# Normalised rows stored by the attention and read through DMA transposes, in a kernel of two recurrent-attention and two gMLP blocks

## The chip, the cores and the metric

One core of one Trainium2 chip. The time is device microseconds (us) of the whole program, the median of its executions. Ratios are the mean time of one kernel's fast runs over that of the other's fast runs of the same rounds on the same chip, so they are not quite the ratio of the medians quoted beside them. The kernel before had medians from 2015 to 2028 us on six occasions, so kernels of different occasions are compared by their ratios to it. Where two kernels are compared stage by stage, that is from one profiled execution of each.

## The reference, cut to what matters

```python
def _A_ref(x, mem0, Wq, Wk, Wv, Wo, seg_len):     # attention over 64 segments of 32 rows, 32 heads of 128
    mem = mem0                                    # 8 memory rows, carried from segment to segment
    for s in range(n_seg):
        h = concat([mem, x[:, 32*s:32*s+32]])
        ...                                       # q, k, v, masked softmax, Wo
        mem = o[:, :M, :].copy()
        outs.append(o[:, M:, :])

def _B_ref(x, w_in, w_sp, b_sp, w_out):           # gMLP: S = 2048 rows, D = 512, F = 1376, Fh = 688
    z = _gelu(einsum('bsd,df->bsf', x, w_in))
    z1 = z[..., :Fh]
    z2 = _layernorm(z[..., Fh:])
    g = einsum('ts,bsf->btf', w_sp, z2) + b_sp
    return einsum('bsf,fd->bsd', z1 * g, w_out)

x = x + _A_ref(_layernorm(x), ...)                # block 1
x = x + _B_ref(_layernorm(x), ...)
x = x + _A_ref(_layernorm(x), ...)                # block 2, the same weights
x = x + _B_ref(_layernorm(x), ...)
```

## The kernel before

TensorE, VectorE and ScalarE run in program order; the order on GpSimd and on SP's DMA queue is a scheduler's. A block is: 64 attention segments; then 16 projections (a row tile of 128 rows is loaded, normalised, transposed, projected to 1376 columns; Gelu on ScalarE; statistics, reciprocal root and normalisation of z2 on VectorE); then 16 gate tiles. The attention's row sums (x plus attention output) are made during later segments, in groups of four row tiles, the last four in the gMLP.

```python
# attention, once per segment s = 4 * tb + j4; `spare` is called ahead of the output product
def spare():
    if ys:
        y_add(ys.pop(0))                               # VectorE: sum, statistics; SP: store to xd
    if tb % 4 == 3 and j4 == 1 and tb > 4:
        due.extend(range(tb - 7, tb - 3))
    if due:
        ys.append(due.pop(0))
        rows.y_load(ys[0], first)                      # SP: 1 + 8 loads for the next sum
    ...
    if j4 == 3 and tb + 2 < NB:
        rows.apply(tb + 2, MV_in, RS_in, first=first)  # VectorE: normalise; SP: 1 store, 4 + 4 reloads
...
# gMLP
def turn_x(tt):
    nc.gpsimd.tensor_scalar(out=_nat(xn[:]), in0=_perm(xt.pop(tt)[:]), ...)        # normalise
    for kt in range(KT):
        nc.tensor.transpose(pT[:, kt * P:(kt + 1) * P], xn[:, kt * P:(kt + 1) * P], ident_bf[:])
    nc.scalar.copy(xnT[tt][:].rearrange("p kt r -> p (kt r)"), pT[:, 0:512])
...
load_x(0); load_x(1)
for t in range(3):
    load_wsp(t)                                        # SP: DMA transposes of w_sp, 128 x 2048 each
turn_x(0)
for tt in range(NT):
    if tt + 2 < NT: load_x(tt + 2)                     # ScalarE's queue
    if tt + 1 < NT: turn_x(tt + 1)
    project(tt)
    if late: late.pop(0)()                             # last four row sums, on GpSimd
    if tt % 2 == 1:
        _rstd_dve(...); normalise(tt - 1); normalise(tt)
...
for t in range(NT):
    gate(t, range(0, 4))                               # each: columns 0:512 and 512:688
    if t > 0: turn_u(t - 1)
    gate(t, range(4, 12))
    if t > 0: finish(t - 1)
    gate(t, range(12, NT))
    product(t)
...
# start
c = _consts(ctx, tc, B_b_sp)                           # GpSimd builds identity and mask, VectorE casts them
...                                                    # then the rows, then the weights (GpSimd's queue)
```

The softmax here doesn't subtract the row's maximum and nothing guards it: scores larger than these inputs give would overflow.

Of the kernel before, what the change touches and what calls it, by code (L numbers as in the profile page):

```python
# [8 lines left out]
F32 = mybir.dt.float32  # L9
# [21 lines left out]
def _perm(ap):  # L31

    return ap.rearrange("p (cg kt el) -> p kt cg el", cg=4, kt=4, el=32)


def _nat(ap):
    return ap.rearrange("p (kt cg el) -> p kt cg el", kt=4, cg=4, el=32)


def _consts(ctx, tc, b_sp):  # L40
# [51 lines left out]
    nc.gpsimd.dma_start(bsp_bf[:], b_sp.rearrange("(t p) -> p t", p=P))  # L92
# [41 lines left out]
class _Rows:  # L134


    def __init__(self, nc, pool, c, xd, xn_d, oA_d, oB_d, x_in):
        self.nc, self.pool, self.c, self.xd, self.xn_d, self.oA_d, self.oB_d, self.x_in = nc, pool, c, xd, xn_d, oA_d, oB_d, x_in
        self.xs, self.preB, self.pre, self.y = {}, {}, {}, {}
# [26 lines left out]
    def y_load(self, tb, first):  # L166
        nc = self.nc
        xs = self.pool.tile([P, DM], BF16 if first else F32, name="y_xb" if first else "y_x")
        nc.sync.dma_start(xs[:], (self.x_in if first else self.xd)[tb * P:(tb + 1) * P, :])
        ot = self.pool.tile([P, 4, P], F32, name="y_o")  # L170
        for j in range(4):
            nc.sync.dma_start(ot[32 * j:32 * j + 24, :, :],
                              self.oA_d[4 * tb + j + 1].rearrange("(cg r) c -> r cg c", cg=4)[8:32])
            r0 = 32 * (tb % 4) + 8 * j
            nc.sync.dma_start(ot[32 * j + 24:32 * j + 32, :, :], self.oB_d[tb // 4, r0:r0 + 8, :].rearrange("r (cg c) -> r cg c", cg=4))
        self.y[tb] = (ot, xs)

    def y_add(self, tb, first, MV, eng):
        ot, xs = self.y.pop(tb)
        o = ot[:].rearrange("p cg c -> p (cg c)")  # L180
        eng.tensor_tensor(out=_perm(o) if first else o, in0=_perm(o) if first else o, in1=_nat(xs[:]) if first else xs[:], op=ALU.add)
        self.nc.sync.dma_start(self.xd[tb * P:(tb + 1) * P, :], o)
        _stats(self.nc, self.pool, o, MV[:, tb, :])


def b_block(tc, c, rows, xd, MV_in, RS_in, MV_out, RS_out, w_in, w_sp, w_out, S, late, out_final=None):
# [4 lines left out]
    with ExitStack() as ctx:  # L191
# [22 lines left out]
        def load_x(tt):  # L214
            xt[tt] = gp.tile([P, DM], F32, name="xs")
            nc.scalar.dma_start(xt[tt][:], xd[tt * P:(tt + 1) * P, :])

        def load_wsp(t):
            wsp[t] = wsp_pool.tile([P, NT, P], BF16, name="wspT")
            nc.sync.dma_start_transpose(out=wsp[t][:], in_=w_sp[t * P:(t + 1) * P, :].rearrange("t (st s) -> t st s", s=P))  # L220

        def turn_x(tt):
            xn = zp.tile([P, DM], BF16, name="xn")
            nc.gpsimd.tensor_scalar(out=_nat(xn[:]), in0=_perm(xt.pop(tt)[:]), scalar1=MV_in[:, tt, 0:1], scalar2=RS_in[:, tt:tt + 1],
                                    op0=ALU.subtract, op1=ALU.mult)
            pT = one.tile([P, 1024], BF16, name="pT")
            for kt in range(KT):
                nc.tensor.transpose(pT[:, kt * P:(kt + 1) * P], xn[:, kt * P:(kt + 1) * P], ident_bf[:])
            xnT[tt] = zp.tile([P, KT, P], BF16, name="xnT")
            nc.scalar.copy(xnT[tt][:].rearrange("p kt r -> p (kt r)"), pT[:, 0:512])  # L230
# [19 lines left out]
        load_x(0)  # L250
        load_x(1)
# [4 lines left out]
        turn_x(0)  # L256
        for tt in range(NT):
            if tt + 2 < NT:
                load_x(tt + 2)
            if tt + 1 < NT:  # L260
                turn_x(tt + 1)
            project(tt)
            if late:
                late.pop(0)()
            if tt % 2 == 1:
                _rstd_dve(nc, zp, RSz[:, tt - 1:tt + 1], MVz[:, tt - 1:tt + 1, 1], 2)
                normalise(tt - 1)
                normalise(tt)
# [6 lines left out]
        def gate(t, sts):  # L275
            if sts[0] == 0:
                pg[t] = big.tile([P, 1536], F32, name="pg")
            for st in sts:
                for c0, c1 in ((0, 512), (512, FH)):
                    nc.tensor.matmul(pg[t][:, c0:c1], lhsT=wsp[t][:, st, :], rhs=z2n[:, st, c0:c1], start=(st == 0), stop=(st == NT - 1))  # L280

        def product(t):
            del wsp[t]
            if t + 3 < NT:
                load_wsp(t + 3)
            u[t] = gp.tile([P, FH], BF16, name="u")
            nc.vector.scalar_tensor_tensor(out=u[t][:], in0=pg.pop(t)[:, 0:FH], scalar=c["bsp"][:, t:t + 1], in1=z1[:, t, :],
                                           op0=ALU.add, op1=ALU.mult)
            load_x(t)
# [10 lines left out]
        def finish(t):  # L300
            py = one.tile([P, DM], F32, name="py")
            for fc, (f0, fsz) in enumerate(FCH):
                nc.tensor.matmul(py[:], lhsT=uT[t][0:fsz, fc, :], rhs=w_out_sb[0:fsz, fc, :], start=(fc == 0), stop=(fc == 5))  # L303
            del uT[t]
            xs = xt.pop(t)
            if out_final is not None:
                xob = gp.tile([P, DM], BF16, name="xob", bufs=1)
                nc.vector.tensor_tensor(out=_nat(xob[:]), in0=_nat(py[:]), in1=_perm(xs[:]), op=ALU.add)
                nc.scalar.dma_start(out_final[t * P:(t + 1) * P, :], xob[:])
                return  # L310
            xo = gp.tile([P, DM], F32, name="xo", bufs=1)
            nc.vector.tensor_tensor(out=_perm(xo[:]), in0=_nat(py[:]), in1=_perm(xs[:]), op=ALU.add)
            nc.scalar.dma_start(xd[t * P:(t + 1) * P, :], xo[:])
            _stats(nc, zp, xo[:], MV_out[:, t, :])
            _rstd_act(nc, RS_out[:, t:t + 1], MV_out[:, t, 1:2], c)
            if t < 2:
                rows.apply(t, MV_out, RS_out, x=xo[:])

        for t in range(NT):
            gate(t, range(0, 4))  # L320
            if t > 0:
                turn_u(t - 1)
            gate(t, range(4, 12))
            if t > 0:
                finish(t - 1)
            gate(t, range(12, NT))
            product(t)
# [5 lines left out]
def kernel(  # L333
# [24 lines left out]
    c = _consts(ctx, tc, B_b_sp)  # L358
# [3 lines left out]
    xn_d = dram.tile([M + S, DM], BF16, name="xn_d")  # L362
    oA_d = dram.tile([S // SEG + 1, P, P], F32, name="oA_d")
# [3 lines left out]
    rows = _Rows(nc, rp, c, xd, xn_d, oA_d, oB_d, x_in)  # L367
    MV, RS = c["MV"], c["RS"]
    with tc.manual_schedule(engines=ORDERED):
# [10 lines left out]
        wqkv = a_open_qkv_weights(tc, ctx, A_Wq, A_Wk, A_Wv)  # L380
        for tt in range(2):
            _stats(nc, rp, rows.xs[tt][:], MV[0][:, tt, :])
            _rstd_act(nc, RS[0][:, tt:tt + 1], MV[0][:, tt, 1:2], c)
            rows.apply(tt, MV[0], RS[0], first=True)
    for blk in range(2):
        late = a_block(tc, c, rows, MV[0], RS[0], MV[1], RS[1], wqkv, A_Wo, S, first=(blk == 0))
        b_block(tc, c, rows, xd, MV[1], RS[1], MV[0], RS[0], B_w_in, B_w_sp, B_w_out, S, late, out_final=out2 if blk == 1 else None)
# [23 lines left out]
def a_block(tc, c, rows, MV_in, RS_in, MV_out, RS_out, wqkv, Wo, S, first):  # L411
# [6 lines left out]
    with ExitStack() as ctx:  # L418
# [123 lines left out]
        def y_add(tb):  # L542
            rows.y_add(tb, first, MV_out, nc.vector)
            copies.append(lambda: _rstd_act(nc, RS_out[:, tb:tb + 1], MV_out[:, tb, 1:2], c))
# [22 lines left out]
        def segment(s, fill, spare):  # L567
# [141 lines left out]
            run(turns)  # L709
            if s + 1 < NSEG:  # L710
                prep_segment(s + 1)
# [9 lines left out]
        for s in range(NSEG):  # L721
# [8 lines left out]
            def spare():  # L730
                if ys:
                    y_add(ys.pop(0))
                if tb % 4 == 3 and j4 == 1 and tb > 4:
                    due.extend(range(tb - 7, tb - 3))
                if due:
                    ys.append(due.pop(0))
                    rows.y_load(ys[0], first)
# [8 lines left out]
            segment(s, lambda: next(more, None), spare)  # L746
# [9 lines left out]
        for tb in ys + due:  # L756
            if tb in due:
                rows.y_load(tb, first)
            y_add(tb)
            run(copies)  # L760


    def late_rstd():
        _rstd_dve(nc, rows.pool, RS_out[:, NB - 4:NB], MV_out[:, NB - 4:NB, 1], 4)

    def step(tb):
        if tb > NB - 4:
            rows.y_add(tb - 1, first, MV_out, nc.gpsimd)
        if tb < NB:
            rows.y_load(tb, first)  # L770

    return [lambda tb=tb: step(tb) for tb in range(NB - 4, NB + 1)] + [late_rstd]
# [35 lines left out]
```

## Time and profile before

| | before |
|---|---|
| time | 2015.21 us (2015.08 to 2018.89) |
| busy: TensorE, VectorE, ScalarE | 89%, 62%, 52% |
| start, to attention segment 0 | 49.4 us |
| attention of block 1, of block 2 | 767.2, 768.3 us |
| projections of block 1, of block 2 (end of the attention's last product to the first gate's product) | 101.1, 102.2 us |
| gates and the turn to block 2; gates of block 2 | 119.2; 109.3 us |

The stages are cut at TensorE's first matmul on the rows of segment 0, at its last matmul of the attention (T), and at VectorE's first product u. The prediction shows the page's lines, the waits and the stage table that this rests on.

Two waits that the prediction did not read matter later, so here they are, from the waits of the whole execution before (total, times, longest):

```profile
DVE y_o L181 <- DMA y_o<-oB_d: 23.2, 3, 11.8
PE psm L452 <- DVE hA L560: 10.8, 12, 1.3
```

VectorE waits for the loads of a row sum (y_o) only three times (a fourth wait of 9.8 us is put down to the store of the attention's output). All four lie where an attention ends (at 810, 823, 1803 and 1812 us), and TensorE's wait for the next segment's rows (hA) is never longer than 1.3 us. So before, row sums don't hold up the segments.

### The profile page before, as it was taken

The numbers are of one execution on the slowest core, as the hardware profiler recorded it, in microseconds if no ns is written. First come the engines' busy times: TensorE is split into PE (matmuls) and PEld (weight loads), VectorE is DVE, ScalarE is ACT, GpSimd is POOL, SyncE is SP. The second block draws the span as 40 slices with busy tenths as digits, with TensorE's granted clock in tenths as the row PEclk, the third lists the DMA queues.
The fourth block names the chain that finished last, engine by engine and source line by source line (L and its number), as shares of the span: only waits on it lengthen the run. The fifth ranks groups of instructions, "written<-read, shape, count | busy, mean of one in ns | idle before, by whom it ended". The sixth has DMA issues, their size and how long they took to land.

```text
span 2016.6 us, 95153 instructions
## 1 busy us (share of the span) xinstructions
PE 1796.6 (89%) x43866; PEld 1027.9 (51%) x43904; DVE 1256.0 (62%) x2835; ACT 1047.8 (52%) x1888; POOL 166.9 (8%) x249
## 2 busy tenths in 40 slices
PE   1999999999999999558989999999999999976798
PEld 0555555555555555224545555555555555542354
DVE  1676777777778766264346676677766777643622
ACT  1566566666666655332236665666666665634311
POOL 5000000000000000440010000000000000014200
PEclk9999999999999999779999999999999999997899
DMA  8200000020012001625540000001200110035153
GB/s 294 77 23 17 19 17 17 24 66 21 17 31 63 18 15 37 176 65 128 150 134 24 20 21 20 20 21 42 65 28 22 56 54 16 16 113 141 52 142 100
DMA packets 163073, 120.09 MB, mean 60 GB/s; under 512 B 97088, under 2 KB 136272, under 8 KB 162672
## 3 DMA queue, kind: packets, MB, share of 16 engines
q1 hardware_dynamic: 141968, 65.71, 12.5%
q10 hardware_dynamic: 13840, 23.08, 3.7%
q0 software_dynamic: 6864, 25.21, 3.5%
q8 instruction: 343, 5.62, 1.2%
q14 instruction: 58, 0.48, 0.1%
HBM read 67.68 MB, written 29.50 MB: 48 GB/s over the span
## 4 chain that ended last, share of the span: by engine, by line
PE 63%; DVE 12%; ACT 10%; DMA 6%; issue 4%; POOL 2%; SPq 1%; DVEq 0%; POOLq 0%; ACTq 0%
PE psm L452 22%; PE pw L509 10%; PE psb L452 8%; PE pg L280 5%; DVE KA L588 5%; ACT rows L584 4%; ACT E L612 3%; PE psO L631 3%; PE psS L608 3%; DVE E L615 3%; PE pwB L518 2%; PE py L303 2%; PE pz L236 2%; DMA xs<-xd 2%; PE psM L675 2%
## 5 line engine op out<-in xcount | busy, mean ns | idle before, releaser
L452 PEld LDWEIGHTS <-hA 128*32 128x32 bf16 x12288 | 308.5, 96 | 307.9 <-DVE hA L560 47.1
L584 ACT CAST rows<-psm 128x512 bf16<-128x512 f32 x512 | 299.7, 585 | 191.2 <-PE psm L452 191.2
L509 PE MATMUL pw<-Wo_sb,uT 128*32 128x128 bf16 x16640 | 267.1, 220 | 32.1 <-issue 21.8
L452 PE MATMUL psm<-Wq_sb,hA 128*32 128x512 bf16 x4096 | 275.3, 384 | 11.3 <-DVE hA L560 10.8
L509 PEld LDWEIGHTS <-uT 128*32 128x32 bf16 x16640 | 245.2, 97 | 72.4 <-issue 33.8
L452 PE MATMUL psm<-Wk_sb,hA 128*32 128x512 bf16 x4096 | 270.4, 381 | 0.0
L452 PE MATMUL psv<-Wv_sb,hA 128*32 128x512 bf16 x4096 | 268.0, 382 | 0.0
L588 DVE STREAM_TRANSPOSE QQ<-rows 128x512 bf16<-128x512 bf16 x256 | 182.1, 711 | 93.3 <-ACT rows L584 92.0
L647 DVE TENSOR_TENSOR uT<-psO,Rt 128x384 bf16<-128x384 f32 x256 | 138.1, 539 | 128.7 <-ACT Rt L637 128.7
L588 DVE STREAM_TRANSPOSE KA<-rows 128x512 bf16<-128x512 bf16 x256 | 182.2, 712 | 40.7 <-ACT rows L584 35.9
L612 ACT ACTIVATE E<-psS 128x448 bf16<-128x448 f32 x256 | 140.0, 547 | 107.6 <-PE psS L608 107.6
L594 DVE CAST VA<-psv 128x512 bf16<-128x512 f32 x256 | 175.6, 686 | 2.3
L553 POOL COPY QQ<-QTB 128x256 bf16<-128x256 bf16 x128 | 51.1, 401 | 1407.9 <-PE psS L608 846.6
L280 PE MATMUL pg<-z2n,wspT 128*128 128x176 bf16 (+1 forms) x1002 | 158.9, 308 | 4.0 <-DVE z2n L247 2.2
L608 PEld LDWEIGHTS <-KA 128*64 128x64 bf16 x2048 | 79.7, 113 | 127.8 <-DVE KA L588 127.4
L637 ACT ACTIVATE Rt<-Rt 128x1024 f32<-128x1024 f32 x128 | 135.3, 1057 | 4.1
L452 PEld LDWEIGHTS <-hB 128*32 128x32 bf16 x3072 | 75.8, 97 | 106.5 <-DVE hB L467 37.3
L636 ACT ACTIVATE Rt<-psD 128x1024 f32<-128x1024 f32 x128 | 128.6, 1004 | 0.0
L692 DVE TENSOR_TENSOR uT<-psO,Rm 128x128 bf16<-128x128 f32 x256 | 62.7, 286 | 92.5 <-PE psO L631 92.4
L608 PE MATMUL psS<-QQ,KA 128*64 128x80 bf16 x2048 | 109.9, 208 | 10.2
L280 PEld LDWEIGHTS <-wspT 128*128 128x128 bf16 x1024 | 85.4, 98 | 65.1 <-issue 9.8
L615 DVE TENSOR_TENSOR E<-E,maskN 128x448 bf16<-128x448 bf16 x256 | 95.0, 371 | 31.4 <-ACT E L612 31.4
(115 smaller groups left out, 2311.7 us busy)
## 6 DMA issues: line engine op xcount, KB each, us to landing
xs<-xd ACTq DMA_DIRECT2D x64, 256.0 KB
oA_d<-o_sb SPq DMA_DIRECT2D x130, 64.0 KB
Wo_sb<-in_A_Wo_dram POOLq DMA_DIRECT2D x8, 1024.0 KB, 13.3
xd<-y_o SPq DMA_DIRECT2D x32, 256.0 KB
y_o<-oA_d SPq DMA_DIRECT2D x128, 48.0 KB
Wq_sb<-in_A_Wq_dram POOLq DMA_DIRECT2D x8, 512.0 KB, 8.2
Wk_sb<-in_A_Wk_dram POOLq DMA_DIRECT2D x8, 512.0 KB, 10.4
xn_d<-ln_xn SPq DMA_DIRECT2D x32, 128.0 KB
```

Of the source, the lines that this page charges most:

```text
L280: nc.tensor.matmul(pg[t][:, c0:c1], lhsT=wsp[t][:, st, :], rhs=z2n[:, st, c0:c1], start=(st == 0), stop=(st == NT - 1))
L452: nc.tensor.matmul(ps[32 * cg:32 * cg + 32, :], lhsT=lhs(kt, cg), rhs=rhs(kt, cg), start=(kt == 0), stop=(kt == KT - 1), tile_position=(0, ...
L509: nc.tensor.matmul(po[32 * cg:32 * cg + 32, 0:128], lhsT=lhs[:, n, :], rhs=wo_rhs(h, cg), start=(h == 0), stop=(h == H - 1), tile_position ...
L584: nc.scalar.copy(r[:], ps[:])
L588: nc.vector.transpose(out=QQ[:, j % 2, :, 0:32] if j < 2 else KA[:, j % 2], in_=r[:])
L594: nc.vector.tensor_copy(VA[:, r].rearrange("p i e -> p (i e)"), ps)
L608: nc.tensor.matmul(pS[64 * g:64 * g + 64, i, c0:80 if K is KA else 112], lhsT=K[:, r, n:n + 2, :].rearrange("p h k -> p (h k)"), rhs=q if ...
L612: nc.scalar.activation(out=E[:, r], in_=pS, func=ACT.Exp, scale=scale)
L615: nc.vector.tensor_tensor(out=E[:, r], in0=E[:, r], in1=maskN[:, j4, :].unsqueeze(1).to_broadcast([P, 4, 112]), op=ALU.mult)
L636: nc.scalar.activation(out=o, in_=in_, func=ACT.Ln)
L637: nc.scalar.activation(out=o, in_=o, func=ACT.Exp, scale=-1.0)
L647: nc.vector.tensor_tensor(out=hview(uT_nxt, 2 * r, 2 * r + 2, 8, 32), in0=oview(2 * r, 2 * r + 2, 8, 32), in1=Rr[:, :, :, 0:24], op=ALU.mult)
```

## The change

Its intent: take GpSimd's normalisation, TensorE's transposes and ScalarE's copies out of the projections, by letting the attention write its rows normalised (xb_d) and reading them transposed by DMA; cut the gate's 688 columns evenly; issue the weights first; make one row tile per segment.

```diff
+    def y_norm(self, tb, MV, RS):
+        self.nc.vector.tensor_scalar(out=_nat(xn[:]), in0=_perm(o), ...)
+        self.nc.sync.dma_start(self.xb_d[tb * P:(tb + 1) * P, :], xn[:])
...
+        def load_xnT(tt):
+            xnT[tt] = zp.tile([P, KT, P], BF16, name="xnT", bufs=3)
+            nc.sync.dma_start_transpose(out=xnT[tt][:], in_=rows.xb_d[tt * P:(tt + 1) * P, :]...)
-        load_x(0)
-        load_x(1)
+        for tt in range(3):
+            load_xnT(tt)
         for t in range(3):
             load_wsp(t)
-        turn_x(0)
+        for tb in (NT - 4, NT - 3):
+            late_load(tb)                    # GpSimd: loads and sum of a late row tile
         for tt in range(NT):
             project(tt)
+            if tt + 3 < NT:
+                load_xnT(tt + 3)
+            if tt in (3, 6):
+                late_norm(NT - 4 + 2 * (tt // 6))   # VectorE: statistics, root, normalise of two
...
-                for c0, c1 in ((0, 512), (512, FH)):
+                for k in range(2):           # columns 344 * k to 344 * k + 344
...
-            gate(t, range(0, 4))
+            gate(t, range(0, 6))
             if t > 0:
                 turn_u(t - 1)
-            gate(t, range(4, 12))
+            gate(t, range(6, 12))
...
-    c = _consts(ctx, tc, B_b_sp)
...
         wqkv = a_open_qkv_weights(tc, ctx, A_Wq, A_Wk, A_Wv)
+        c = _consts(ctx, tc, B_b_sp)
...
             def spare():
                 if ys:
-                    y_add(ys.pop(0))
-                if tb % 4 == 3 and j4 == 1 and tb > 4:
-                    due.extend(range(tb - 7, tb - 3))
-                if due:
-                    ys.append(due.pop(0))
-                    rows.y_load(ys[0], first)
+                    y_add(ys[0])
...
+            def tail():                      # called at the segment's end, behind rows.apply
+                if ys:
+                    rows.y_norm(ys.pop(0), MV_out, RS_out)
+                if tb % 4 == 3 and j4 == 0 and tb > 4:
+                    due.extend(range(tb - 7, tb - 3))
+                if due:
+                    ys.append(due.pop(0))
+                    rows.y_load(ys[0], first, nc.sync)
```

Cut from the diff: the load of b_sp on ScalarE's queue, the buffer counts of u and xo, the last row tile of the attention's group behind its last segment, the calls of load_x, turn_x and late that leave the loop, and the loads of the last two late row tiles, which are called at tt = 3.

## The prediction

> **What bounds the kernel now.** I read the page first, to see in which slices TensorE isn't full, then busy time by stage, then the waits of the bad stages, then the timeline of their edges.
>
> ```profile
> PE   1999999999999999558989999999999999976798
> PEclk9999999999999999779999999999999999997899
> ```
>
> TensorE is full in both attention blocks and sags in three places: the start, and slices 17-18 and 37-38, where each gMLP projects its rows. The stage table says how much (columns: stage, length, busy time of PE, PEld, DVE, ACT, POOL with counts, clock, DMA share, GB/s):
>
> ```profile
> 817.00:911.30 94.30, 51.97 (x251) 24.97 (x257) 44.35 (x163) 36.60 (x56) 39.85 (x22) 0.78 0.38 106
> 918.60:1027.50 108.90, 101.62 (x642) 53.23 (x652) 36.96 (x62) 20.14 (x60) 0.00 (x0) 1.00 0.56 144
> 1907.30:2009.80 102.50, 100.51 (x648) 53.80 (x658) 25.32 (x31) 12.68 (x30) 0.00 (x0) 1.00 0.50 122
> ```
>
> The projections take 94.3 us with no engine above 55%, at a granted clock of 0.78; the gate stages (2nd and 3rd line) are PE-bound. So the projections are a chain of waits. The waits of 816-912 us (total, times, longest) name its links:
>
> ```profile
> POOL xn L224 <- DMA xs<-xd: 46.3, 11, 9.8
> PEld L228 <- POOL xn L224: 46.3, 12, 9.2
> DVE bnst L130 <- POOL y_o L181: 20.7, 4, 7.0
> ACT z L239 <- DVE z2n L247: 18.1, 2, 9.2
> ```
>
> Row tile load, normalise on GpSimd (2.07 us each), transpose on PE, copy on ACT, project: one tile at a time, because the load of tile t+2 stands in ACT's queue behind the Gelus of tile t. The last four rows' sums are woven in, on GpSimd, and VectorE waits for them in order. Block 2 (1805-1908 us) shows the same pairs within some 20%.
>
> The third place is the start:
>
> ```profile
> 13.38 0.87 SPq L373 DMA_DIRECT2D x<-in_A_x_dram  x2
> 18.35 0.67 DVE L130 BATCH_NORM_STATS2 bnst<-x 128x6 f32<-128x512 bf16 x1
> 37.32 1.90 PE L452 MATMUL psb<-Wq_sb,hB 128*32 128x512 bf16 x16 [37.32 <-DVE hB L467]
> 37.68 0.53 POOL L407 DMA_DIRECT2D Wv_sb<-in_A_Wv_dram  x1 [0.86 <-DMA Wk_sb<-in_A_Wk_dram]
> 49.39 1.95 PE L452 MATMUL psm<-Wq_sb,hA 128*32 128x512 bf16 x16
> ```
>
> The rows are read only at 13.38 (their buffers lie over the constants' scratch), the first matmul starts at 37.32, then PE waits for Wv: segment 0 starts at 49.39.
>
> **What the Trainium skill says.** (1) "TensorE: Matmul & The Clock Gate", section "Wait - 56ns, not 53.3ns?": a warm matmul of N columns takes N/2.4 GHz + about 2.5 ns. For 688 columns in two pieces that is 291.7 ns, however they are cut. The trace agrees: 8 row tiles of the gate, 16 matmuls, take 2.34 us (1021.06 to 1023.40), 292.5 ns a pair. (2) The same page, "Part 1: The HAM clock gate": the clock is half after about 3.4 us of idleness, and full again after as long a busy stretch. It agrees: 12 projection matmuls take 4.29 us after a wait, else 2.49 us. (3) "ScalarE: Activation LUTs", "What ACT_TABLE_LOAD costs": 1283 ns; the trace has 1.28 us, and around the first two tiles of each gMLP five such loads, because a Ln and an Exp stand between Gelus. (4) "DMA: Bandwidth & Descriptors", "DMA Transpose (X-bar)": only SP or ACT may issue it, on 2-byte data, and two issuing streams must not overlap. The change keeps all on SP, as before. No latency for a 128x512 transpose is in this trace; the 128x2048 ones hold SP 1.93 to 6.97 us at issue.
>
> **The change, part by part.** The diff doesn't show the order, so I compared the built programs.
>
> *Projections.* T is the end of the last matmul of the attention's last product (816.57; 1805.15 in block 2). Before, the first projection starts at T+9.9 (826.45; 1814.99) and gate 0 ends at T+101.0 (its product starts at 917.63) and T+102.1 (1907.34).
> After, rows 0 to 11 lie normalised in DRAM. But the first transposed load waits for that same last matmul, since xnT lies over Wo. Hence about 0.1 wait + 0.6 issue (a quarter of 2.5) + 2.5 to land (estimate): first projection at T+3.3. PE has then been idle about 3.3 us, so I take one cold tile and a half (4 us, 3.3 us), later 2.3 us (8 x 0.216 + 4 x 0.149).
> Then VectorE becomes the bound. From compact stretches of the trace: statistics of one tile 1.09 (880.82 to 881.91), the reciprocal root of a pair 2.21 (842.55 to 844.76), two normalisations 1.11. A pair costs 2 x 1.09 + 2.21 + 1.11 = 5.5, sixteen tiles 44 us. The late rows add, in VectorE's fixed order after tiles 3 and 6, two statistics (1.7), a root (2.2) and two normalisations (1.1, from 0.546 for the same form): 5.0 each, 10 us. First statistics at T+8, last normalisation 44+10 later plus waits. Stepping through the order with z2's three buffers:
> - Late row sums on GpSimd: about 9 DMA issues a tile at some 0.52 us, 2.3 to land, 1.15 to add. I get T+11.8 and T+18.3 for the first two, in time; T+30.9 and T+36.5 for the others, the last costing VectorE 2.6 us.
> - PE waits for Gelus, these for z2 buffers: stalls before tiles 7 and 11.
> - Last normalisation at T+67. Gate 0 catches up with it: end at T+67.3.
> I add 3 us for contention of GpSimd's adds with VectorE and for the transposed w_sp loads that precede the fourth xnT load in SP's queue: T+70. Gain 31 + 32 = 63 us. The 128 transposes leave PE and the 32 copies ACT; they lay inside waits, so nothing more is counted.
>
> *Gates.* The balanced columns: 0 by (1). Two more row tiles ahead of the transposes of u hide its latency. In block 1 a period is 7.01 us, in block 2 6.76: VectorE does statistics ahead of the product in block 1. These lines show the wait (periods 8.18, 7.01):
>
> ```profile
> 926.79 0.62 PE L294 MATMUL pT<-ident_bf,u 128*128 128x128 bf16 x6 [1.28 <-DVE u L287]
> 934.97 0.62 PE L294 MATMUL pT<-ident_bf,u 128*128 128x128 bf16 x6 [1.28 <-DVE u L287]
> 941.98 0.62 PE L294 MATMUL pT<-ident_bf,u 128*128 128x128 bf16 x6
> ```
>
> Gain 12 x 0.25 + 2 x 0.6 = 4.2; block 2 none, as it waits for nothing. I say 4.5 for small change at its tail.
>
> *Start.* Here I expect a loss. The weights are issued 9 us earlier, but GpSimd now does the constants after all 24 issues, and VectorE, in order, casts the identity and the mask before it touches the rows. Issue 24 waits for load 16: 3 + 16 x 1.44 (the pace of 20.37 to 37.68) = 26; the constants took 9.0 less a DMA of 1.4, so 34; one Wo issue and two selects: mask at 35.6, 1.8 of memsets, statistics at about 38 (before: 18.35). The old distance from there to the first matmul was 19 us with the queues full; now Wo's 4 MB keep them full to about 49, so 13: first matmul near 51. Wv is there by then, so the block projections run through, 6 us: segment 0 at 57 against 49.4, less some 3 us that segment 0 lost to the cold clock. +5, between 0 and 10.
>
> *Attention.* Eleven normalisations of 0.55 us a block go into segment tails on VectorE, the twelfth behind the last segment. Where no block projection is turned there, VectorE idles 1.13 us, and it costs nothing. Where it is, the slack is 0.15, so about 0.2 in 12 segments: +2.5.
>
> Sum: 2015.2 - 63 - 4.5 + 5 + 2.5 = 1955.
>
> **The rivals.** (a) *Transposes are slow*: an xnT load queues behind 1.5 MB of w_sp on SP and PE waits a tile or more. For it: SP's 8.03 us for two w_sp loads. Against: that queue is full only at the fourth tile; VectorE paces the rest. +5 a block: 1965. (b) *Late rows decide*: GpSimd issues some 40 DMAs by software, and one slip of 5 us goes straight through VectorE's order. For it: 20.7 us of exactly this wait before. 1965 to 1980. (c) *PE becomes the bound*: if VectorE's small steps were cheaper than I read, the projections would end near T+50, and the time were 1915. Against: their durations are measured and serial. (d) *No loss at the start*: weights 9 us earlier, segment 0 at 41: 1941. Against: the built order puts VectorE's statistics behind the mask.
>
> **Range and chances.** The projections' uncertainty is about 8 us a block and mostly common to both, the start 5: 1936 to 1978. Faster by 2% means under 1975: 0.86; within 2%: 0.13; slower 0.01.
>
> **What would show it.** Right: the wait of VectorE on ACT's Gelus shrinks and VectorE is over 75% busy in the projections; gate 0 ends 65 to 75 us after the last attention matmul; ACT has no table loads between Gelus; first matmul of the kernel later than 45 us; gate periods of block 1 at 6.8 us, of block 2 unchanged at 6.76. Wrong: xnT waits of many us in the middle of the projections, VectorE below 60% there, a first matmul before 37 us, or attention segments longer by over 0.3 us on average.

## The result, and the profile after

The changed kernel took 1997.61 us (1990.84 to 1999.21; before beside it 2017.05), ratio 0.989, 95% interval 0.985 to 0.993. The second time it was run the ratio was 0.987. That is a gain of 1.1 to 1.3%, and the predicted range, 1936 to 1978 us, is missed by some 20 us. All outputs are correct.

From one profile of each (span 2016.6 before, 1989.1 after; the profiled execution of after was the fastest of its four, so the stages add up to 27.5 us, where the ratios make it 22 us for the first set of runs and 27 for the second):

| stage | before | after | difference | predicted |
|---|---|---|---|---|
| start, to segment 0 | 49.39 | 61.53 | +12.1 | +7.6 |
| segment 0 of block 1 | 14.29 | 11.32 | -3.0 | -3 |
| the rest of the attention, block 1 | 752.9 | 759.2 | +6.3 | +1.2 |
| projections, block 1 | 101.1 | 75.7 | -25.4 | -31 |
| gates, and the turn to block 2 | 119.2 | 116.7 | -2.6 | -4.2 |
| attention, block 2 | 768.3 | 777.6 | +9.3 | +1.2 |
| projections, block 2 | 102.2 | 78.5 | -23.6 | -32 |
| gates, block 2 | 109.3 | 108.6 | -0.6 | -0.3 |
| sum | | | -27.5 | -60 (rounded there) |

Of the 32 us missing, 14 are in the projections, 13 in the attention, 4 to 5 in the start, and one or two in the gates. The page after shows the same by its slices (TensorE's busy tenths, then the granted clock):

```profile
PE   0899999999998999769989999999899989986798
PEclk9999999999999999979989999999999999998899
```

Against the line of before, the hollow of slices 17 and 18 is less deep (7 and 6, once 5 and 5), but slice 1 is a 0, and in the attention stand 8s (slices 13, 29 and 33) where there were 9s.

**Start.** The timeline of the first 66 us after: VectorE's casts of the constants, the first row statistics, TensorE's first matmul of the block's rows and of segment 0. In brackets stands how long the engine sat idle, and what ended it.

```profile
29.92 0.31 DVE L52 CAST ident_bf<-ident_f 128x128 bf16<-128x128 f32 x1 [25.97 <-POOL ident_f L49]
37.85 0.40 DVE L76 CAST maskN<-maskf 128x448 bf16<-128x448 f32 x1 [7.62 <-POOL maskf L73]
40.14 0.69 DVE L130 BATCH_NORM_STATS2 bnst<-x 128x6 f32<-128x512 bf16 x1
54.15 1.90 PE L473 MATMUL psb<-Wq_sb,hB 128*32 128x512 bf16 x16 [54.15 <-DVE hB L488]
61.53 1.05 PE L473 MATMUL psm<-Wq_sb,hA 128*32 128x512 bf16 x16
```

The mechanism is the predicted one: VectorE idles 26 us for GpSimd's identity, which now comes behind 24 weight issues, and touches the rows at 40.14 instead of 18.35.

**Attention.** The waits of the execution after, the counterparts of the two lines shown for before:

```profile
DVE y_o L180 <- DMA y_o<-oB_d: 32.8, 6, 9.2
PE psm L473 <- DVE hA L582: 26.6, 16, 5.0
```

VectorE's wait for a row sum's loads rose from 3 times to 6, of which two are again at the end of an attention, and TensorE now waits up to 5.0 us for a segment's rows. I measured all 128 segments, from the first matmul on one segment's rows to that on the next. Apart from segment 0 of each block, most differ by less than 0.6 us, some in block 2 by up to 1.2 us, in both directions. Segments 32/33 and 48/49 of each block stand out in one direction, all but segment 33 of block 1: 13.8 + 12.2 and 15.0 + 13.7 us in block 1, 16.3 + 14.2 and 16.7 + 14.3 in block 2, where before had 11.6 to 12.4. Against the same segments of before that is +7.2 and +13.6, together 20.8 us; the gains elsewhere hide a part of it in the table. The timeline around segment 32 of block 2 shows why. SPq is SP's DMA queue: start, time that it holds the queue, destination and source.

```profile
1404.71 2.61 SPq L156 DMA_DIRECT2D preB<-xn_d  x4
1407.37 2.18 SPq L163 DMA_DIRECT2D pre<-xn_d  x4
1409.66 0.41 SPq L587 DMA_DIRECT2D oA_d<-o_sb  x1
1410.59 0.40 SPq L173 DMA_DIRECT2D y_o<-oA_d  x1
1414.18 0.30 SPq L175 DMA_DIRECT2D y_o<-oB_d  x1
1415.94 0.69 DVE L180 TENSOR_TENSOR y_o<-y_o,y_x 128x512 f32<-128x512 f32 x1 [4.79 <-DMA y_o<-oB_d]
1418.64 0.31 DVE L582 STREAM_TRANSPOSE hA<-pre 128x128 bf16<-128x128 bf16 x1
1419.01 1.90 PE L473 MATMUL psm<-Wq_sb,hA 128*32 128x512 bf16 x16 [4.62 <-DVE hA L582]
```

The loads of the row sum (first and last shown) stand behind the eight reloads of the next row tile (preB, pre) and a store. They land at 1415.9; VectorE, in order, has stood for 4.79 us at the sum, and the rows of the next segment (hA) come behind it. TensorE idles 4.62 us and then runs at half the clock for a while: 1.90 us for what takes 1.05. (At the four places TensorE idles 2.1, 3.3, 4.6 and 5.0 us.) Before, in the same segment, the order is the other one:

```profile
1421.63 0.30 SPq L175 DMA_DIRECT2D y_o<-oB_d  x1
1421.98 2.62 SPq L156 DMA_DIRECT2D preB<-xn_d  x4
1424.64 2.18 SPq L163 DMA_DIRECT2D pre<-xn_d  x4
1425.43 0.69 DVE L181 TENSOR_TENSOR y_o<-y_o,y_x 128x512 f32<-128x512 f32 x1
```

The last of the sum's loads is issued ahead of preB, and the sum waits for nothing. The change moved the call of the loads from `spare`, ahead of `rows.apply`, to `tail`, behind it; with one buffer of y_o and the normalisation reading it, it had to stand behind the latter. Only the segments with j4 = 3 have an `apply`, so one sum in four is hit. The Trainium skill's "Perfetto Trace Analysis", section "DMA Instruction — HWDGE (DVE, Sync)", says that the sequencer first waits for a DMA's semaphores, then makes its descriptors, and only then is free for the next instruction. The trace agrees: behind an entry that waits or is slow to issue, everything later in SP's queue is late. Here SP stood still for 2.7 us ahead of the reloads (1402.0 to 1404.7), and then needed 4.8 us to issue them.

**Projections.** The stage table after (columns as in the prediction):

```profile
832.02:907.68 75.66, 50.75 (x223) 24.20 (x227) 52.02 (x197) 25.42 (x37) 26.90 (x42) 0.82 0.47 112
1801.96:1880.50 78.54, 51.04 (x222) 24.20 (x227) 53.40 (x200) 24.25 (x36) 27.05 (x42) 0.80 0.52 115
```

VectorE is busy 52 and 53.4 us, as the prediction's sum of 54 has it, but the stage is 22 to 25 us longer than that (16 were predicted), so it is 69 and 68% busy, between the prediction's sign for right (75%) and its sign for wrong (60%). The timeline of block 1:

```profile
835.76 8.81 PE L252 MATMUL pz<-w_in_sb,xnT 128*128 128x512 bf16 x35 [3.73 <-issue]
837.05 10.46 SPq L246 DMA_TRANSPOSE wspT<-in_B_w_sp_dram  x3
847.62 3.82 SPq L229 DMA_TRANSPOSE xnT<-xb_d  x3
850.44 11.05 PE L252 MATMUL pz<-w_in_sb,xnT 128*128 128x512 bf16 x47 [5.87 <-DMA xnT<-xb_d]
855.38 0.52 DVE L258 BATCH_NORM_STATS2 bnst<-z 128x6 f32<-128x344 f32 x1 [6.59 <-ACT z L255]
868.38 1.17 POOL L180 TENSOR_TENSOR xo<-xo,xs 128x512 f32<-128x512 f32 x1
868.42 1.16 DVE L124 SCALAR_TENSOR_TENSOR ny<-nq,nb 128x2 f32<-128x2 f32 x1
```

Three transposed loads of w_sp hold SP for 10.46 us. The fourth row tile's transposed load stands behind them, TensorE waits 5.87 us for it, and VectorE, the engine that sets the stage's length, loses 6.59 us (6.71 in block 2). This is the prediction's rival (a). The other idle times of VectorE between its first statistics at 840.52 (T + 8.5, predicted T + 8) and the last normalisation are 1.31, 0.28, 0.19 and 1.80 us, the last for a late row sum on GpSimd. The last two lines show one more us: a small VectorE instruction took 1.16 us instead of 0.16, because GpSimd's sum of two SBUF tiles began 0.04 us earlier. The Trainium skill's "SBUF — State Buffer", section "SBUF: two separate sides", says that VectorE with two SBUF inputs and GpSimd lock a port pair for a whole instruction; the trace agrees with that.

### The profile page after: what moved, and what is told of

Read it like the earlier page. It is cut to its first block, busy times and chain, and to the rows that moved or that the text cites. A ratio compares the mean times of both kernels' runs of the same rounds, so it can differ in the third digit from the quotient of the medians.

```text
span 1989.1 us, 94885 instructions
## 1 busy us (share of the span) xinstructions
PE 1784.2 (90%) x43752; PEld 1033.4 (52%) x43776; DVE 1273.2 (64%) x2891; ACT 1023.4 (51%) x1848; POOL 139.2 (7%) x288
## 3 DMA queue, kind: packets, MB, share of 16 engines
q1 hardware_dynamic: 158864, 70.43, 13.8%
## 4 chain that ended last, share of the span: by engine, by line
PE 36%; DVE 9%; ACT 4%; issue 2%; DMA 2%; SPq 2%; POOL 1%; DVEq 0%; POOLq 0%; ACTq 0%
PE psm L473 12%; PE pg L298 6%; PE pw L530 5%; PE psb L473 4%; DVE KA L610 2%; PE py L323 2%; ACT rows L606 2%; ACT E L634 2%; PE psO L653 2%; PE psS L630 1%; DVE E L637 1%; PE pwB L539 1%; PE psM L697 1%; PE psD L706 1%; PE pT L314 1%
## 5 line engine op out<-in xcount | busy, mean ns | idle before, releaser
L298 PE MATMUL pg<-z2n,wspT 128*128 128x344 bf16 x1024 | 160.7, 310 | 5.0 <-DVE z2n L263 4.8
L252 PE MATMUL pz<-w_in_sb,xnT 128*128 128x512 bf16 (+1 forms) x376 | 91.7, 409 | 47.5 <-ACT z L256 24.9
L298 PEld LDWEIGHTS <-wspT 128*128 128x128 bf16 x1024 | 95.3, 98 | 57.9 <-issue 12.6
```

Of the source, the lines that this page charges most:

```text
L252: nc.tensor.matmul(pz[:, c0:c1], lhsT=xnT[tt][:, kt, :], rhs=w_in_sb[:, kt, c0:c1], start=(kt == 0), stop=(kt == KT - 1))
L298: nc.tensor.matmul(pg[t][:, k, 0:344], lhsT=wsp[t][:, st, :], rhs=z2n[:, st, 344 * k:344 * k + 344], start=(st == 0), stop=(st == NT - 1))
```

## The experiments

Twelve runs. "Changed" is the changed kernel; the first four runs were on one chip.

### e_after_again: the changed kernel again

> The changed kernel, unaltered, as the yardstick of the three runs beside it on the same chip. In its first profile the median was 1997.6 us and the ratio to before 0.989 with a wide interval. If that was not an odd run: 0.985 to 0.993 again; segment 0 starts near 61.5 us, segments 32/33 and 48/49 of the attention are long again (13.8+12.2 and 15.0+13.7 us in block 1), and the projections stall some 6.6 us for the fourth transposed load. If the first run was odd: another ratio, and the long segments at other places.

Measured: 1996.99 us, ratio 0.9865 (0.983 to 0.990). Segment 0 at 61.60; segments 32/33 and 48/49 at 14.1 + 12.0 and 15.1 + 14.0 us in block 1, 16.9 + 13.9 and 15.9 + 14.3 in block 2; VectorE's wait for tile 3 6.20 us in block 1, in block 2 even 12.61. The projections of block 2 took 82.7 us here. So the places are the same, and the first result was not odd.

### e_start_back: the constants ahead of the weights again

```diff
+    c = _consts(ctx, tc, B_b_sp)          # ahead of the rows, as before
...
-        c = _consts(ctx, tc, B_b_sp)      # behind the weight issues
-    nc.scalar.dma_start(bsp_bf[:], ...)
+    nc.gpsimd.dma_start(bsp_bf[:], ...)
```

> The changed kernel with the constants built ahead of the rows and weights, as before. Theory (the constants, once behind the weight issues, hold VectorE back from the row statistics): first matmul at 37 us instead of 54, segment 1 starts near 63.7 instead of 72.9, time 9 us less than the changed kernel. Rival (the start waits for the weights' bytes whatever the order, or the loss is made good later): less than 3 us.

Measured: 1989.41 us, ratio 0.9818 (0.980 to 0.984), first matmul at 37.72, segment 1 at 63.53. That is 7.6 us by the medians, 9.5 by the ratios, 9.4 at segment 1. The start of the change costs what the theory says.

### e_skip: no row-sum loads in a segment with reloads

```diff
-                if due:
+                if due and not (j4 == 3 and tb + 2 < NB):
```

> The changed kernel, with one edit: no row tile is loaded for the sums in a segment that also normalises and reloads the next row tile. Theory (in such a segment the 8 loads stand in SP's queue behind the 8 reloads of the next rows, so they land after VectorE asks for them in the next segment): the wait of VectorE for y_o from oB_d falls from 32.8 us to about 17 (only the one behind the last segment of each block stays), segments 32/33 and 48/49 come back to 11.6 to 12.4 us, and the time falls by 18 to 21 us. Rival (the normalisation itself on VectorE, or the clock, makes the attention longer): the segments stay long or the loss spreads, under 5 us gained.

Measured: 1976.06 us, ratio 0.9763 (0.973 to 0.980): 20.9 us less by the medians. Its waits:

```profile
DVE y_o L180 <- DMA y_o<-oB_d: 16.0, 2, 9.1
PE psm L473 <- DVE hA L582: 11.5, 12, 1.0
```

Only one wait is left behind each block's last segment, and TensorE's wait is back at its size of before. Segments 32/33 and 48/49 take 11.6 to 12.3 us, and the attentions 763.3 and 764.1 us, 21 less than in the run beside it. The normalisations are still in the segments, so they are not what made the attention longer: behind segment 0 that of block 1 takes 752.0 us, against 752.9 before. The rival falls.

### e_wsp_late: the first w_sp loads behind later row tiles

```diff
-        for t in range(3):
-            load_wsp(t)
...
+            if tt in (6, 8, 10):
+                with tc.issue_after(turned[tt + 3].ins):   # behind row tile tt + 3 in SP's order
+                    load_wsp((tt - 6) // 2)
```

(The dependency is there because, as I read the built order, the scheduler puts a load without one back to the front of SP's queue. No run shows that.)

> The changed kernel, with the first three transposed w_sp loads put behind the row tiles 9, 11 and 13 in SP's queue instead of ahead of the fourth. Theory (VectorE is the bound of the projections and loses 6.6 us a block because tile 3 comes late; nothing else takes the place of that wait): 12 us less than the changed kernel, the projection stage 75.7 to 69 us, VectorE above 85% busy in it. Rival (the late rows on GpSimd, or the Gelus waiting for z2 buffers, take the place of the wait): under 5 us. A further risk: the first gate then waits for its w_sp tile.

Measured: 1985.86 us, ratio 0.9803 (0.977 to 0.983): 11.1 us less by the medians. The stage table:

```profile
834.40:908.00 73.60, 49.00 (x226) 23.62 (x226) 53.30 (x200) 25.49 (x37) 26.59 (x42) 0.83 0.49 116
1795.20:1867.50 72.30, 49.31 (x226) 23.63 (x226) 52.60 (x198) 23.99 (x36) 27.12 (x42) 0.85 0.51 125
```

The wait for tile 3 is gone in both blocks, and the gates wait for no w_sp tile. The time is as the theory has it, the stage isn't: 73.6 and 72.3 us instead of 69, and VectorE is 72 to 73% busy, not 85. Of its idle time, 8.7 and 8.4 us lie ahead of the first statistics (T + 12.1 and T + 10.0, where the changed kernel had T + 8.5 in block 1), and 2.6 and 2.3 us are for a late row on GpSimd. Where the first projection loses its time is told with e_all2.

### e_newton2: two Newton steps

```diff
-    for k in range(3):
+    for k in range(2):
...
```

> The changed kernel with two instead of three Newton steps in the reciprocal root on VectorE: 3 small instructions, 3 x 0.196 = 0.59 us, less in each of 10 roots of a block (correctness should hold: the error after two steps is some 5e-6). Theory (VectorE, in order, is the bound of the projections from tile 3 on): 9 of 10 roots of a block lie there, so 2 x 9 x 0.59 = 10.6 us less than the changed kernel, and the stage 75.7 to about 70 us. Rival (Gelus, PE or the late rows on GpSimd pace the stage, and the small steps fill gaps): under 3 us.

Measured: 1983.63 us, ratio 0.9819 (0.978 to 0.986), correct. Against the changed kernel's 0.9865, on another chip, that is some 9 us, with intervals that overlap. In the profile VectorE's busy time of the stage falls by 5 us (47.1 and 47.5 where the changed kernel run again had 52.2 and 52.3), and the stage of block 1 from 75.0 to 71.8 us, while VectorE's wait for the last late row grows from 1.4 to 3.7 us. So VectorE sets the pace, but GpSimd's late rows are close behind and take a part of what it gains: the expected 70 us are not reached. Block 2 took 77.5 us, of which 12.4 are the wait for tile 3.

### e_stats_first: row statistics ahead of the constants

```diff
...
+    rows_first(c)                          # statistics, root and normalisation of row tiles 0 and 1
     ident_f = tmp.tile([P, P], F32, name="ident_f")
     nc.gpsimd.memset(ident_f[:], 0.0)
```

> The changed kernel, with the statistics and normalisation of the first two row tiles put ahead of the constants in VectorE's order (weights are still issued first). Theory (the weights first are right, only VectorE's order spoils it): row statistics near 10 us instead of 40, first matmul near 37, all of Wv there by 41, segment 1 starts at 56 to 60 us instead of 72.9, so 13 to 17 us less than the changed kernel and some 4 to 7 less than with the constants first. Rival (the rows' way through memory is held up by 16 MB of weights in the queues as long as before): segment 1 near 64, 9 us less, as with the constants first.

Measured: 1983.41 us, ratio 0.9813 (0.977 to 0.986). The timeline of its start:

```profile
4.80 0.68 DVE L132 BATCH_NORM_STATS2 bnst<-x 128x6 f32<-128x512 bf16 x1
26.48 1.90 PE L478 MATMUL psb<-Wq_sb,hB 128*32 128x512 bf16 x16 [26.48 <-DVE hB L493]
39.56 0.62 PE L478 MATMUL psb<-Wv_sb,hB 128*32 128x512 bf16 x4 [0.72 <-DMA Wv_sb<-in_A_Wv_dram]
41.32 1.94 PE L478 MATMUL psm<-Wq_sb,hA 128*32 128x512 bf16 x16
```

The first matmul came earlier than I expected (26.48), then TensorE waits for Wv piece by piece; segment 1 starts at 57.39, inside the expected 56 to 60, 15.5 us ahead of the changed kernel and 6.1 ahead of e_start_back. Segment 1 itself takes 1.9 us longer than in the changed kernel, so that 13.6 us are left at segment 2. So at the start weights first is right, and what spoils it is one engine's order: VectorE stood in front of casts that the first rows don't need. The whole time shows less: by the ratios it is 10 us under the changed kernel, on another chip, where 13 to 17 were expected, and not distinguishable from e_start_back (0.9813 against 0.9818), where 4 to 7 were.

### e_b_cols: only the columns, in the kernel before

```diff
-                for c0, c1 in ((0, 512), (512, FH)):
+                for k in range(2):         # 344 * k to 344 * k + 344
...
```

> The kernel before, with the gate's columns cut into 344 and 344 instead of 512 and 176, and nothing else. Theory of the prediction (a matmul's time goes by its columns, the sum is the same): time as before within 1 us, gate periods 7.01 and 6.76 us as before. Rival (balanced pieces hide the weight loads better, as the change intends): periods shorter by 0.1 us or more, that is 3 us or more in all.

Measured: 2017.17 us, ratio 0.9975 (0.995 to 1.000). The gate periods are 7.01 us in block 1 (from the fifth on) and 6.76 in block 2, within 0.01 us as before, so the even cut is worth nothing. The interval alone would not have shown that.

### e_b_split: only the split of the gate, in the kernel before

```diff
-            gate(t, range(0, 4))
+            gate(t, range(0, 6))
-            gate(t, range(4, 12))
+            gate(t, range(6, 12))
```

> The kernel before, with 6/6/4 instead of 4/8/4 row tiles of the gate around the transposes of u and the output product, and nothing else. Theory of the prediction (in block 1 VectorE's statistics push the product of u behind, and two more row tiles hide that): periods of block 1 fall from 7.01 to 6.76 or a little less, the first two by 0.6 us, 4.2 us in all; block 2 stays at 6.76. Rival (the gain of the changed kernel's gates comes from the columns or from the buffers of u and xo): periods of block 1 stay at 7.01.

Measured: 2020.87 us, ratio 0.9986 (0.996 to 1.002). The time does not resolve it: in this profile the projections of block 2, which the edit does not touch, took 114 us instead of 102. The timeline of TensorE's transposes of u does, from e_b_split and, behind the cut, from e_b_cols:

```profile
990.63 0.61 PE L294 MATMUL pT<-ident_bf,u 128*128 128x128 bf16 x6
997.36 0.61 PE L294 MATMUL pT<-ident_bf,u 128*128 128x128 bf16 x6
```

```profile
992.34 0.62 PE L296 MATMUL pT<-ident_bf,u 128*128 128x128 bf16 x6
999.35 0.62 PE L296 MATMUL pT<-ident_bf,u 128*128 128x128 bf16 x6
```

6.73 us a period against 7.01; the first two periods fall from 8.18 to 7.6, and block 2 from 6.76 to 6.72. From the first to the last transpose of u block 1 gains 5.1 us here, 5.8 in the changed kernel. So the gain of the changed kernel's gates is that of the split.

### e_two: both waits taken away

The edits of e_skip and e_wsp_late together.

> The changed kernel with both waits taken away that the prediction had not seen: no row tile loaded in a segment that reloads the next rows, and the first w_sp loads behind row tiles 9, 11 and 13. Theory (the two are independent, and with the start's loss they are all that separates the prediction from the result): the gains add, 21 + 10 us, so 1965 us (0.970 of before); the segments 32/33 and 48/49 at 11.6 to 12.4 us and the projections at 72 to 74 us a block. Rival (what one wait gives back the other takes, or the loss sits elsewhere): above 1975 us.

Measured: 1967.69 us, ratio 0.9723 (0.970 to 0.975). Segments 32/33 and 48/49 take 11.6 to 12.3 us; the projections 70.8 and 76.2 us, the second above what I expected. In block 1 that is 7.3 us less than with e_skip alone (78.1), so the wait for the fourth row tile (8.5 us there) costs most of its length. The gains add. With these two waits away, the time lies in the range of the prediction. (Its text says that the prediction had not seen both; the second it had named, as rival (a), and set aside.)

### e_all: four repairs

The edits of e_skip, e_wsp_late, e_newton2 and e_stats_first together.

> The changed kernel with all four repairs: the two of the run before this one, two Newton steps, and the row statistics ahead of the constants. If the four are independent: 21 + 10 + 9 + 13 us less than the changed kernel, 1942 us, 0.961 of before. If they overlap (a faster VectorE only meets the late rows on GpSimd, or the next wait): 1950 to 1960 us.

Measured: 1950.58 us, ratio 0.9631 (0.961 to 0.965). Most of it adds; 4 us are missing by the ratio, whose interval just reaches the expected 0.961, and 8 by the median. The projections took 71.5 and 74.2 us, although VectorE had 5 us less to do than in e_two. The first projection came 6.9 and 6.0 us behind T. And VectorE now waits for late rows, 8.0 us in block 1 and 8.3 in block 2, where e_two had 3.4 and 3.7. The longest wait of each block (xo is a late row tile):

```profile
857.84 0.69 DVE L132 BATCH_NORM_STATS2 bnst<-xo 128x6 f32<-128x512 f32 x1 [6.24 <-POOL xo L182]
1795.44 0.69 DVE L132 BATCH_NORM_STATS2 bnst<-xo 128x6 f32<-128x512 f32 x1 [6.08 <-DMA xs<-xd]
```

This is the overlap that the expectation named: a faster VectorE meets the late rows.

### e_b_start: only the start, in the kernel before

```diff
-    c = _consts(ctx, tc, B_b_sp)           # ahead of the rows
...
+        c = _consts(ctx, tc, B_b_sp)       # behind the weight issues
```

> The kernel before, with only the start of the change: constants behind the weight issues, the load of b_sp on ACT's queue. Theory (this part alone loses 9 us net: segment 0 starts 12 us later, runs 3 us faster as the clock is up by then): segment 1 starts at 72.9 instead of 63.7 us and the ratio to before is 1.0045. Rival (weights first is neutral or good without the rest of the change): ratio 1.000 or less, segment 1 at 64 us or earlier.

Measured: 2035.15 us, ratio 1.0056 (1.003 to 1.009), segment 0 at 61.02, segment 1 at 72.33. Alone, this part makes the kernel slower, by the expected amount within the interval.

### e_all2: a fifth repair, the first transposed loads ahead of a store

In e_two, block 2 (timeline; the attention's last matmul ended at 1777.02):

```profile
1777.54 0.69 DVE L180 TENSOR_TENSOR y_o<-y_o,y_x 128x512 f32<-128x512 f32 x1 [10.23 <-DMA y_o<-oB_d]
1778.26 0.34 SPq L181 DMA_DIRECT2D xd<-y_o  x1
1778.78 2.64 SPq L229 DMA_TRANSPOSE xnT<-xb_d  x2
1784.70 5.48 PE L252 MATMUL pz<-w_in_sb,xnT 128*128 128x512 bf16 x14 [7.68 <-issue]
```

The last row sum of the attention waits 10 us for its loads (that these are late because of w_in's bytes, as the expectation says, was not tested), and the first transposed load stands behind that sum's store in SP's queue: the same fault a third time.

```diff
         for tt in range(3):
             load_xnT(tt)
+        with tc.issue_after(turned[1].ins):
+            last()                         # the last sum, its store, its normalisation
```

> The kernel with the four repairs, and a fifth: the first two transposed row tiles stand ahead of the store of the last row sum in SP's queue (that sum waits for rows that arrive behind the 1.4 MB of w_in). Theory (the first projection came 3.7 to 7.7 us behind the end of the attention because SP, in order, held the first transposed load behind that store): it comes at 3.3 to 4 us in both blocks, some 5 us in all less than with four repairs: 1945 us, 0.960 of before. Rival (the transposed loads themselves queue behind w_in's bytes): the first projection stays at 6 us and the ratio at 0.963.

Measured: 1940.73 us, ratio 0.9597 (0.957 to 0.962), correct. From its timeline of block 1 (the attention's last matmul ended at 811.02):

```profile
811.06 2.62 SPq L231 DMA_TRANSPOSE xnT<-xb_d  x2
814.61 5.60 PE L254 MATMUL pz<-w_in_sb,xnT 128*128 128x512 bf16 x14 [3.59 <-issue]
815.77 0.45 SPq L183 DMA_DIRECT2D xd<-y_o  x1
```

The first projection comes 3.6 us behind T in block 1 and 4.7 in block 2, which misses the expected 4 there, and the projections take 67.3 and 72.8 us. VectorE's first statistics gain less: T + 10.5 against T + 12.3 in e_all in block 1, and nothing in block 2 (T + 11.5 both times). One cause is in the timeline: ScalarE's table load, 1.28 us, now comes behind the first projection (at 819.43 in block 1) and not ahead of it. In block 1 the rest of the gain is a shorter wait for late rows (4.9 us after 8.0); in block 2 it is still 8.3. This is the fastest version: 4.0% under the kernel before, and 2.7 to 3% under the changed one by their ratios to before (not taken on the same chip). Its gain over e_all is by ratios from two chips whose intervals just overlap; the shift of the first projection is shown by the profile, that the time fell by this shift is not.

## Why the prediction was wrong, point by point

**Direction and bound: right.** The projections were a chain of waits, the change takes the chain away, and VectorE becomes the bound: its busy time came out at 52 to 53 us where the prediction summed 54, and e_newton2 shows that less work on it shortens the stage. The table loads between Gelus and the transposes are gone.

**Attention, "+2.5": the step that failed in kind.** The prediction counted VectorE's time for the new normalisations in segment tails and nothing else. It did not ask what the move of the row-sum loads from `spare` to `tail` does to SP's queue. In one segment of four they now queue behind eight reloads, and VectorE's fixed order turns 2.3 to 5.2 us of lateness into a stop of TensorE, which the colder clock makes longer. Cost: 20.8 us at four places, shown by e_skip, which gets 20.9 back by one condition; for the normalisations themselves it shows no cost. The prediction's own counter-sign, "attention segments longer by over 0.3 us on average", would not have caught it: the mean is 0.1 us, the loss sits in 7 of 128 segments.

**Projections, "Gain 31 + 32": right in mechanism, mis-sized.** Measured 25.4 + 23.7. The term "I add 3 us for contention ... and for the transposed w_sp loads" is the one: the w_sp loads alone cost VectorE 6.6 and 6.7 us, and up to 12.6 in a second execution. I had named this as rival (a), had seen 1.93 to 6.97 us per issue in the trace of before, and set it aside with "that queue is full only at the fourth tile; VectorE paces the rest", at 5 us a block. But the fourth tile is needed early: TensorE was through with three tiles 9 us after it had begun, and SP was held until 847.5, 12 us after. A transposed row load itself held SP 1.2 us, not the 0.6 that I scaled from the larger ones. e_wsp_late gets 11.1 us back. So one of the prediction's own signs of being wrong came true ("xnT waits of many us in the middle of the projections"). In block 2 the first projection also came at T + 6.05 us, where T + 3.3 was predicted, behind the last sum's store; e_all2 puts it forward, but shows no earlier statistics for it in block 2.

**Late rows (rival b): in part, and mis-sized.** They cost 1.3 to 1.8 us a block in the changed kernel. But in block 1 their sums were ready at T + 17.2, 23.7, 37.5 and 43.9 us, where the prediction stepped to T + 11.8, 18.3, 30.9 and 36.5. That was hidden, because the wait for the fourth tile made VectorE late too. With that wait gone they cost 3 to 4 us a block (e_wsp_late, e_two), and up to 8.3 where VectorE also has less to do (e_all, e_all2). So they are the next wait to take away.

**Start, "+5": right in mechanism, too small.** Measured +9.1 net (+12.1, and -3.0 for segment 0's clock). The mask was ready at 37.85 against 35.6 predicted, the way from the statistics to the first matmul took 14.0 us against 13, and from there to segment 0 7.4 against 6, since TensorE began cold. e_start_back and e_b_start show the 9 us with both kernels, and e_stats_first that VectorE's order is its cause.

**Gates, "4.2" and columns "0": right.** The columns are worth nothing (e_b_cols), in the changed kernel the span from the first to the last transpose of u in block 1 falls by 5.8 us (108.89 to 103.08; by 5.1 with the split alone), more than predicted, because its third and later periods fell to 6.72 and not 6.76 and one period of 8.44 went to 7.09. At the turn to block 2, 2.7 us were lost again: TensorE ran the first matmuls of the new block at half the clock (1.90 us where before had 1.05). That does not belong to the change: from the last transpose of u to segment 0 this turn takes 12.03 us in e_b_cols and e_b_start too, which leave it as before, and 9.34 in e_wsp_late, e_newton2 and e_two, which have the change. TensorE's gaps ahead of it are the same in all runs (1.28, 0.78 and 1.09 us). What decides between the two stays open. Why the first two periods still take 7.6 us was not followed either.

**The sum.** Attention 13, projections 14, start 4 and gates 1 us make up the 32 that are missing. The waits that the prediction had summed were those of the engines; the two largest that it missed or made too small were in the queue of an engine that computes nothing, and there they were common to both blocks, so the range could not average them out.

## What to carry to other kernels

When a change moves a call, follow its DMA issues in the issuing queue and not only its instructions on the engines: a load is as late as everything ahead of it, and an engine with a fixed order passes that on to work that has nothing to do with it. Put slow issues without hurry, like large transposed loads, behind the small ones that someone waits for, and check in the built order that the scheduler left them there. Moving bulk loads to the front of a program pays only if nothing that the first rows need comes to stand behind them in an engine's order.

## What the Trainium skill lacked or had wrong

- "DMA: Bandwidth & Descriptors", section "Issuing engines are not separate DMA queues", calls the time to initiate a DMA "usually small relative to the DMA itself". For the DMA transposes here it was long enough to decide the stage: three of 128x2048 held SP for 10.46 us, and one of 128x512 for 1.20 us. Its section "DMA Transpose (X-bar)" gives conditions, but no such times by size.
- No page that I read draws the consequence of the order in "Perfetto Trace Analysis" (wait, then descriptors, then the next instruction): one entry that waits for its data, or is slow to issue, holds all later loads of that queue. Here a store put the first projection of block 2 at T + 7.7 (e_two) instead of T + 4.7 us (e_all2), and eight reloads cost the attention 20.8 us at four places.
- "TensorE: Matmul & The Clock Gate", "Part 1: The HAM clock gate", puts the fall to half the clock after an idle window of about 3.4 us. The case above fits (after 4.62 us of idleness, 16 matmuls took 1.90 us instead of 1.05). But at the turn to block 2, with gaps of 1.28, 0.78 and 1.09 us and matmuls between them, the first 16 matmuls ran at about half the clock in 9 of the 14 profiles (1.85 to 1.90 us) and at the full one in 5 (1.05 us). The section gives no measure for such short gaps.
